# Attention by pairs of heads: two 64-row or two 64-column products at a time, values unsplit float32, scores in float32r from the ninth pair on

## The chip, the cores and the metric

The kernel runs on one core of a Trainium2 chip. The metric is the device time of one execution in microseconds (us), the median of several runs. In the rows below PE is the matrix engine (TensorE), PEld its loads of stationary operands, DVE the vector engine, ACT the scalar engine, POOL the GpSimd engine and SP the engine that issues the DMAs.

## What is computed

Attention over 4 batches of 8 heads, 576 positions of 64 elements, with a mask in blocks of 64, and then two feed-forward layers on the 2304 tokens. The second and third step are not touched by the change.

```python
scores = scale * np.matmul(q, k.transpose(0, 1, 3, 2))
mask = block_i >= block_j                      # blocks of 64 positions
attn = softmax(np.where(mask, scores, -1e9))
x = np.matmul(attn, v)                         # heads side by side: 2304 x 512
x = (silu(x @ w_gate) * (x @ w_val)) @ w_out   # 512 -> 1536 -> 512
out = elu(x @ w_in) @ w_out2                   # 512 -> 2048 -> 512
```

## The kernel before

The tokens are cut into nine chunks of 256. Chunk 0 holds the first 64 positions of each batch; each other chunk holds 256 query positions of one batch (`ORDER`). With g = 0 a chunk's queries see 320 keys, with g = 1 they see 576, so the 32 pairs of heads of chunks 1 to 8 are 16 pairs of the short kind (g = 0) and 16 of the long kind (g = 1), by turns four and four.

PE takes operands in two types here: float32, for which the trace shows two loads and two matmul records for each product, and float32r, for which it shows one. A float32r product keeps fewer bits, so a number is split into a high float32r part and the float32r rest, and the parts are multiplied separately (`mm3` is the three-product form of the feed-forward layers, L183 to L185).

**Attention of one head** (`a_head`) before. Heads 0 to 7 (`fp`) use float32: scores on 64 rows of the array (L476), values on 64 columns (L590, and L614 for the last 64 keys). Heads 8 to 63 use float32r on the whole array: the high part and the rest of the keys are stacked in the 128 rows (`ks`), so that two products, with `qh` and `ql`, make a score block (L478, L479); the high part and the rest of the values stand side by side in the 128 columns (`vs`), so that two products, with the parts `th` and `tl` of the transposed probabilities, make a values step of 128 keys (L592, L593), and one product the last 64 keys (L616). A block of scores is masked, its maximum taken, exponentiated and divided by its sum (DVE, ACT); the probabilities are transposed on PE (L575, L576, L603) and copied out by ACT (L580), split on DVE (L584). `xb`, `xf`, `xh` and `xl` add the two halves of the result and split them for the next layer.

**What runs beside it.** `gv_pair` is the first feed-forward layer of a chunk: 12 slices of 24 products of 256 columns (L183 to L185, written `gv`). Its weights are read as raw words and converted by `conv_unit` on ACT, DVE and POOL. From about 490 us on the other layers follow (`y`, then `h` and `o`).

**What sets the order.** Every step is a task with a guessed duration and a priority; `Plan.order` runs a list schedule over them and emits the instructions of each engine in the order that it finds. Each engine then runs its own list strictly in that order. A task has a `whole` mark: where PE changes between marks, the plan adds `SWITCH` ns to the task and holds the change back by `STAY`. `UNIT0`, `UNIT`, `LEAD1`, `LEAD2` and `LEAD` set when chunks and their heads fall due. `NFILL` zero products (L274) fill PE at the start.

Of the kernel before, what the change touches and what calls it, by code (L numbers as in the profile page):

```python
# [8 lines left out]
F32 = mybir.dt.float32  # L9
# [25 lines left out]
UNIT0, UNIT, LEAD1, LEAD2, LEAD, CLEAD, CSTEP = 3.4, 3.4, 35.0, 10.0, 22.0, 16.0, 1.0  # L35
GF, NACT, NFP, XLP = 4, 48, 8, False
NPOOL = ()
# [4 lines left out]
STAY, SWITCH, HOLD = 30.0, 100.0, 250.0  # L42
# [86 lines left out]
def attention_moe_moe_kernel(ctx: ExitStack, tc: tile.TileContext,  # L129
                             q0, k0, v0, qf, kf, qt, kt, va, vb, wg, wv, wo, w2i, w2o, out):  # L130
# [82 lines left out]
    def sc_lo():  # L213
        return at_ps.tile([128, 512], F32, tag="slo", name="slo")

    def sc_hi():
        return at_ps.tile([128, 2, 512], F32, tag="shi", name="shi")

    cur = {}

    def tr_t():
        cur["tr"] = at_ps.tile([128, 512], F32, tag="tr", name="tr", bufs=2)
        return cur["tr"]

    def pv_t():
        return at_ps.tile([128, 512], F32, tag="pv", name="pv")


    plan = Plan(dict(raw=3, rawb=2, c=4, rk=2, rq=2, rv=2, ks=3, qh=2, ql=2, vs=3, nm=3, sm=3, pl0=2, pl1=2, ph=2, th=3, tl=3,
                     tt=2, xb=2, xf=2, x=3, slo=1, shi=1, tr=2, pv=1, gv=2, th1=2, s2=2, st=2,  # L230
                     ar=5, ah=3, y=6, ys=4, ws=NW, wm=3, gp=NP, et=2, hc=4))
# [3 lines left out]
    pl_t = {g: [attn.tile([128, e], F32, name=f"pl{g}{i}") for i in range(2)] for g, e in ((0, 256), (1, 512))}  # L235
    ph_t = [attn.tile([128, S], F32, name=f"ph{i}") for i in range(2)]
# [32 lines left out]
    def t0_fill():  # L269
        zeros = [nc.const_aps.tensor(0.0, (128, n), F32).bitcast(F32R) for n in (128, 256)]  # L270

        def fill():
            t = cur["tr"] if "tr" in cur else tr_t()
            pe.matmul(t[:, 256:512], zeros[0], zeros[1], start=True, stop=True)  # L274

        add("DVE", 300, lambda: None, PT0 - 1, writes=[("wt", 0, 0)])
        for n in range(NFILL):
            add("PE", 107, lambda n=n: [fill() for _ in range(1 if n else 3)], PFILL, [("wt", 0, 0)])
# [4 lines left out]
    def t0_init():  # L283
# [4 lines left out]
        for i in range(2):  # L288
            add("POOL", 190, lambda i=i: pool.memset(pl_t[0][i][:, 192:256], 0.0), PT0, writes=[("plz", 0, i)])
            add("POOL", 190, lambda i=i: pool.memset(pl_t[1][i][:, 448:512], 0.0), PT0, writes=[("plz", 1, i)])  # L290
# [17 lines left out]
    def t0_attn(s, q):  # L308
        tag = ("slo", "pv", "shi", "shi")[2 * s + q]
        sc_k, tr_k, pv_k = (tag, plan.count["shi"] if s and q else nxt(tag), q), ("tr", nxt("tr"), 0), ("gv", nxt("gv"), 0)  # L310
        st, hs, n = {}, range(4 * q, 4 * q + 4), f"0{s}{q}"

        def qk():
            if s == 0:
                t = (sc_lo, pv_t)[q]()
            else:
                if "t" not in t0_sc:
                    t0_sc["t"] = sc_hi()
                t = t0_sc["t"][:, q]
            st["sc"] = t[:, 0:256].rearrange("p (h k) -> p h k", h=4)  # L320
            for h in hs:
                pe.matmul(st["sc"][:, h % 4], qz[s][:, h], kz[s][:, h], start=True, stop=True)
# [75 lines left out]
    NH = B * 2 * H  # L398
    raws, xfs = {}, {}

    def a_pair(n, prio):
        b, g = ORDER[n // H]
        h, i = n % H, n // 2
        ext, nf = (320, 2) if g == 0 else (576, 4)
        fp = n < NFP

        def lk():
            t = raws.setdefault(i, {})[0] = attn.tile([128, 2, S], F32, tag="rk", name="rk", bufs=2)
            if fp:
                sp.dma_start(out=t[:, 0, 0:ext], in_=kf[h // 2])  # L410
            else:
                sp.dma_start(out=t[:, :, 0:ext], in_=kt[b, :, h:h + 2, 0:ext])

        def lq():
            t = raws.setdefault(i, {})[1] = attn.tile([128, 2, QW], F32, tag="rq", name="rq", bufs=2)
            if fp:
                sp.dma_start(out=t[:, 0], in_=qf[h // 2])
            else:
                sp.dma_start(out=t, in_=qt[g, b, :, h:h + 2])

        def lv():
            rv = raws.setdefault(i, {})[2] = attn.tile([128, 5, 128], F32, tag="rv", name="rv", bufs=2)
            sp.dma_start(out=rv[:, 0:nf + 1], in_=(va, vb)[g][b, h // 2])

        add("SP", 450, lk, prio, [], [("rk", i, 0)], data=500 if fp else 3.0 * ext)
        add("SP", 450, lq, prio, [], [("rq", i, 0)], data=420 if fp else 730)
        add("SP", 450, lv, prio, [], [("rv", i, 0)], data=200 * (nf + 1))

    def a_head(n, prio):
        b, g = ORDER[n // H]  # L430
        h, j, i = n % H, n % 2, n // 2
# [3 lines left out]
        K = {k: (k, n, 0) for k in ("ks", "qh", "ql", "vs", "nm", "sm", "tt", "xb")}  # L435
        K["ksl"], K["vsl"] = ("ks", n, 1), ("vs", n, 1)
        rk, rq, rv = ((k, i, 0) for k in ("rk", "rq", "rv"))

        def new(k, *shape, bufs, dt=F32R):
            st[k] = attn.tile(list(shape), dt, tag=k, name=k, bufs=bufs)  # L440
            return st[k]

        def p_ks():
            act.copy(new("ks", 128, S, bufs=3)[:, 0:ext], raws[i][0][:, j, 0:ext])  # L444

        def p_ksl():
            pool.tensor_tensor(st["ks"][64:128, 0:ext], raws[i][0][64:128, j, 0:ext], st["ks"][64:128, 0:ext].bitcast(F32), ALU.subtract)  # L447

        def p_qh():
            act.copy(new("qh", 128, QW, bufs=2), raws[i][1][:, j])  # L450

        def p_ql():
            pool.tensor_tensor(new("ql", 128, QW, bufs=2), raws[i][1][:, j], st["qh"].bitcast(F32), ALU.subtract)

        def p_vs():
            act.copy(new("vs", 128, 5, 128, bufs=3)[:, 0:nf + 1, 0:64], raws[i][2][:, 0:nf + 1, 64 * j:64 * j + 64])  # L456

        def p_vsl():
            v = st["vs"][:, 0:nf + 1]
            pool.tensor_tensor(v[:, :, 64:128], raws[i][2][:, 0:nf + 1, 64 * j:64 * j + 64], v[:, :, 0:64].bitcast(F32), ALU.subtract)  # L460

        fp, us = n < NFP, slice(64 * j, 64 * j + 64)
        if not fp:
            add("ACT", .833 * ext + 93, p_ks, prio, [rk], [K["ks"]])
            add("POOL", 2.1 * ext + 250, p_ksl, prio, [rk, K["ks"]], [K["ksl"]])
            add("ACT", 307, p_qh, prio, [rq], [K["qh"]])
            add("POOL", 790, p_ql, prio, [rq, K["qh"]], [K["ql"]])
            add("ACT", .833 * 64 * (nf + 1) + 93, p_vs, prio, [rv], [K["vs"]])
            add("POOL", 2.1 * 64 * (nf + 1) + 230, p_vsl, prio, [rv, K["vs"]], [K["vsl"]])
        qk_in = [rk, rq] if fp else [K["ks"], K["ksl"], K["qh"], K["ql"]]  # L470
        v_in = [rv] if fp else [K["vs"], K["vsl"]]

        def qk(v, t, o, w):
            qs = slice(128 * t, 128 * t + 128)
            if fp:
                pe.matmul(v, raws[i][1][us, 0, qs], raws[i][0][us, 0, o:o + w], start=True, stop=True)  # L476
            else:
                pe.matmul(v, st["qh"][:, qs], st["ks"][:, o:o + w], start=True, stop=False)  # L478
                pe.matmul(v, st["ql"][:, qs], st["ks"][:, o:o + w], start=False, stop=True)  # L479

        slo, shi = ("slo", nxt("slo"), 0), ("shi", nxt("shi"), 0)

        def nm_t():
            if "nm" not in st:
                new("nm", 128, 2, bufs=3, dt=F32)
            return st["nm"]

        def sm_t():
            if "sm" not in st:
                new("sm", 128, 2, bufs=3, dt=F32)  # L490
            return st["sm"]

        def qk_lo():
            sc = st["slo"] = sc_lo()[:, 0:e0]
            qk(sc, 0, 0, e0)

        def qk_hi():
            sc = sc_hi()
            if e1 <= 512:
                vw, st["ax"] = [(sc[:, 0, 0:e1], 0)], AXX  # L500
                st["shi"] = sc[:, 0, 0:e1]
            else:
                w = e1 // 2
                vw, st["ax"] = [(sc[:, u, 0:w], w * u) for u in range(2)], AXXY
                st["shi"] = sc[:, :, 0:w]
            st["hi_end"] = vw[-1][0]
            for v, o in vw:
                qk(v, 1, o, v.shape[-1])

        def mask(v):  # L510
            w = v.shape[-1]
            dve.memset(v[0:64, w - 64:w], NEG)

        def mx(u):
            v, ax = (st["slo"], AXX) if u == 0 else (st["shi"], st["ax"])
# [661 lines left out]
```

## Time and profile before

| | |
|---|---|
| median of 3 runs | 1021.86 us (1021.21 to 1023.21) |
| the profiled execution, its own time | 1022.86 us |
| its span, first to last instruction | 1021.1 us |
| PE busy | 1010.5 us (99%), 6542 matmul records |
| DVE busy | 742.6 us (73%) |
| ACT busy | 652.6 us (64%) |
| POOL busy | 285.2 us (28%) |
| granted clock of PE | 1.00 of full speed in the whole span |

A matmul's duration in the profile covers its way through the array: a `gv` product of 256 columns is shown as 0.28 us long, while the next one starts 0.11 to 0.12 us after it. What a product costs PE is therefore read from one start to the next, not from its duration, and a wait shorter than the overlap doesn't show as idle time.

### The profile page before, as it was taken

The page shows a single profiled execution, that of the slowest core. Times are in us where ns is not written, and L with a number is a line of the kernel's source. Part 1 is how long each engine was busy: PE and PEld are TensorE (multiplying, and loading weights), DVE is VectorE, ACT ScalarE, POOL GpSimd, SP SyncE. Part 2 cuts the span into 40 slices and gives each one's busy share as a digit, 9 for nine tenths or more (in the row PEclk, how much of TensorE's full clock was granted, in tenths as well). Part 3 has the DMA queues.
Part 4 walks back from the last instruction along what each step waited for, and adds up shares of the span by engine and source line. Part 5 has one row for each costly group of instructions (what it writes and reads, how often), then busy time and mean ns, then how long its engine had stood idle before and what let it go on. Part 6 is the DMA issues. An engine that isn't in the chain of part 4 may idle for free.

```text
span 1021.1 us, 19137 instructions
## 1 busy us (share of the span) xinstructions
PE 1010.5 (99%) x6542; PEld 930.3 (91%) x6542; DVE 742.6 (73%) x1813; ACT 652.6 (64%) x1645; POOL 285.2 (28%) x291
## 2 busy tenths in 40 slices
PE   9999999999999999999999999999999999999998
PEld 7789999999999999999888889889889989899997
DVE  7899988777777788878766955786986454754554
ACT  6898889888888677653455554655564444654443
POOL 3467535433443344323333322232200000000000
PEclk9999999999999999999999999999999999999999
DMA  6766454323432343015797886887656334353431
GB/s 215 237 209 222 151 180 151 102 84 104 135 115 73 105 125 101 32 64 176 254 340 261 296 323 232 268 264 219 203 155 200 120 114 124 117 176 121 122 105 62
DMA packets 90896, 169.94 MB, mean 166 GB/s; under 512 B 9008, under 2 KB 35120, under 8 KB 90800
## 3 DMA queue, kind: packets, MB, share of 16 engines
q1 hardware_dynamic: 90800, 168.73, 51.5%
q8 instruction: 52, 0.85, 0.4%
q14 instruction: 44, 0.36, 0.1%
HBM read 130.42 MB, written 38.27 MB: 165 GB/s over the span
## 4 chain that ended last, share of the span: by engine, by line
PE 82%; DVE 8%; ACT 4%; DMA 3%; issue 2%; SPq 0%; ACTq 0%; DVEq 0%
PE gv L183 8%; PE gv L184 8%; PE gv L185 7%; PE o L939 6%; PE o L937 6%; PE o L938 6%; PE h L183 5%; PE h L185 5%; PE h L184 5%; PE y L184 5%; PE y L185 5%; PE y L183 5%; PE pv L593 2%; PE pv L592 2%; PE tr L575 2%
## 5 line engine op out<-in xcount | busy, mean ns | idle before, releaser
L183 PE MATMUL gv<-xh,wh 128*128 128x256 f32 x864 | 255.3, 296 | 0.6 <-DVE as L687 0.4
L184 PE MATMUL gv<-xl,wh 128*128 128x256 f32 x864 | 241.3, 279 | 0.0
L185 PE MATMUL gv<-xh,wl 128*128 128x256 f32 x864 | 241.0, 279 | 0.0
L183 PEld LDWEIGHTS gv<-xh,wh 128*128 128x128 f32 x864 | 162.9, 189 | 4.2 <-issue 2.5
L184 PEld LDWEIGHTS gv<-xl,wh 128*128 128x128 f32 x864 | 163.2, 189 | 0.2
L185 PEld LDWEIGHTS gv<-xh,wl 128*128 128x128 f32 x864 | 162.9, 188 | 0.0
L183 PE MATMUL h<-yo,ws 128*128 128x384 f32 x336 | 113.8, 339 | 2.6 <-ACT ys L902 1.2
L185 PE MATMUL h<-yo,ws 128*128 128x384 f32 x336 | 112.8, 336 | 0.0
L184 PE MATMUL h<-yo,ws 128*128 128x384 f32 x336 | 112.7, 335 | 0.0
L898 DVE TENSOR_TENSOR ys<-h,ys 128x384 f32<-128x384 f32 x72 | 40.0, 555 | 68.6 <-ACT ys L902 42.9
L184 PE MATMUL y<-al,woh 128*128 128x512 f32 (+1 forms) x240 | 88.2, 367 | 0.0
L185 PE MATMUL y<-ah,wol 128*128 128x512 f32 (+1 forms) x240 | 88.2, 367 | 0.0
L183 PE MATMUL y<-ah,woh 128*128 128x512 f32 (+1 forms) x240 | 88.2, 367 | 0.0
L848 POOL TENSOR_TENSOR wm<-c,wm 128x256 fp32r<-128x256 f32 x56 | 51.2, 922 | 127.6 <-ACT wm L845 127.5
L891 DVE SCALAR_TENSOR_TENSOR ar<-ar,ar 128x384 f32<-128x384 f32 x96 | 56.5, 589 | 35.3 <-ACT ar L890 34.8
L902 ACT COPY ys<-h 128x384 f32<-128x384 f32 x72 | 34.3, 476 | 74.4 <-PE h L185 73.9
L584 DVE TENSOR_TENSOR tl<-tr,th 128x256 fp32r<-128x256 f32 x176 | 68.9, 415 | 12.0 <-ACT th L580 11.6
L460 POOL TENSOR_TENSOR vs<-rv,vs 128x320 fp32r<-128x320 f32 (+1 forms) x56 | 43.4, 777 | 122.2 <-ACT vs L456 88.6
L889 ACT ACTIVATE ar<-ys 128x384 f32<-128x384 f32 x72 | 37.8, 526 | 59.6 <-DVE ys L898 34.6
L183 PEld LDWEIGHTS h<-yo,ws 128*128 128x128 f32 x336 | 63.1, 188 | 12.1 <-DVE ys L898 3.2
L447 POOL TENSOR_TENSOR ks<-rk,ks 64x576 fp32r<-64x576 f32 (+1 forms) x56 | 68.6, 1226 | 16.4 <-ACT ks L444 7.0
L580 ACT CAST th<-tr 128x256 fp32r<-128x256 f32 x176 | 60.3, 377 | 17.9 <-PE tr L576 16.2
(156 smaller groups left out, 2737.8 us busy)
## 6 DMA issues: line engine op xcount, KB each, us to landing
ws<-w_scr SPq DMA_DIRECT2D x168, 256.0 KB, 2.6
w_scr<-wm SPq DMA_DIRECT2D x56, 256.0 KB, 3.9
a_scr<-as SPq DMA_DIRECT2D x54, 256.0 KB, 2.5
ar<-a_scr SPq DMA_DIRECT2D x48, 256.0 KB, 4.7
rk<-in_kt_dram SPq DMA_DIRECT2D x16, 576.0 KB, 4.1
raw<-in_w2i_dram SPq DMA_DIRECT2D x16, 512.0 KB, 5.3
raw<-in_w2o_dram SPq DMA_DIRECT2D x16, 512.0 KB, 5.1
rq<-in_qt_dram SPq DMA_DIRECT2D x28, 256.0 KB, 3.6
```

The lines of the kernel that those rows point to most:

```text
L183: pe.matmul(dst, wh, xh, start=start, stop=False, skip_group_check=more)
L184: pe.matmul(dst, wh, xl, start=False, stop=False, skip_group_check=more)
L185: pe.matmul(dst, wl, xh, start=False, stop=stop, skip_group_check=more)
L447: pool.tensor_tensor(st["ks"][64:128, 0:ext], raws[i][0][64:128, j, 0:ext], st["ks"][64:128, 0:ext].bitcast(F32), ALU.subtract)
L460: pool.tensor_tensor(v[:, :, 64:128], raws[i][2][:, 0:nf + 1, 64 * j:64 * j + 64], v[:, :, 0:64].bitcast(F32), ALU.subtract)
L580: act.copy(st["th", c], st["tr", c][:, 0:QW])
L584: dve.tensor_tensor(st["tl", c], st["tr", c][:, 0:QW], st["th", c].bitcast(F32), ALU.subtract)
L848: add("POOL", 1000, lambda: pool.tensor_tensor(wm[n][:, 1], part(*x), wm[n][:, 0].bitcast(F32), ALU.subtract), prio, [ck(*x), hk] + whole, ...
L891: add("DVE", 575, lambda: dve.scalar_tensor_tensor(t(), e(), 1.0, t(), ALU.add, ALU.mult), PMP, [tk, ek], [tk])
L937: pe.matmul(d, h, OH[f], start=(p == 0 and u < 2), stop=False)
L938: pe.matmul(d, h, OL[f], start=False, stop=False)
L939: pe.matmul(d, l, OH[f], start=False, stop=(p == HP - 1 and u > 1))
```

## The change

Attention is done by pairs of heads, head 0 of a pair in rows or columns 0 to 63 of the array, head 1 in 64 to 127, their products by turns.

- Keys, queries and values of a pair are loaded once, the two heads over each other (64 rows each) or side by side (64 columns each). The doubled keys and queries in DRAM go.
- **Scores** (`qk` in `a_pair`): for pairs 0 to 7 one float32 product for each block and head; from pair 8 on (`QS`) three float32r products (`qh*kh`, `qh*kl`, `ql*kh`), all on 64 rows. A pair's scores are one task: 4 products (short) or 6 (long) of float32, 12 or 18 of float32r. The blocks of the long kind are 512, 64 and 448 columns wide, of the short kind 320 and 192.
- **Values** (`pv` in `a_pair`): float32 for all pairs, on 64 columns, 6 (short) or 10 (long) products in one task. The last step has 128 columns and covers 128 keys, of which the first 64 meet zeros.
- The splits of the values (`vs`) and of the transposed probabilities (`tl`, `tt`), and `xb` and `xf`, go; keys and queries are split once for a pair. The division by the sum goes from ACT (heads 0 to 47) to DVE. Two steps of transposed probabilities are copied out at once (512 columns).
- Buffers: scores in `sa` and `sb` (1024 columns each), transposes and values share `tp` (two of 512).
- The numbers of the plan: `UNIT` 3.4 to 3.6, the leads, `STAY` 30 to 10. Transposes now come after all the zero products.

```diff
-UNIT0, UNIT, LEAD1, LEAD2, LEAD, CLEAD, CSTEP = 3.4, 3.4, 35.0, 10.0, 22.0, 16.0, 1.0
-GF, NACT, NFP, XLP = 4, 48, 8, False
+UNIT0, UNIT, LEAD1, LEAD2, LEAD, CLEAD, CSTEP = 3.6, 3.6, 25.0, 40.0, 40.0, 20.0, 0.8
+GF, NACT, NTH, QS, NRV = 4, 0, 6, 8, 3
-STAY, SWITCH, HOLD = 30.0, 100.0, 250.0
+STAY, SWITCH, HOLD = 10.0, 100.0, 250.0
...
+        pieces = [(0, 1, 0, 320), (320, 0, 0, 192)] if g == 0 else [(0, 1, 0, 512), (512, 1, 512, 64), (576, 0, 0, 448)]
...
+            for t, (at, q, o, w), j in [(t, p, j) for p in pieces for t in range(len(terms)) for j in range(2)]:
+                us, qs, (x, y) = slice(64 * j, 64 * j + 64), slice(128 * q, 128 * q + 128), terms[t]
+                pe.matmul(sc[j][:, at:at + w], raw[x][us, qs], raw[y][us, o:o + w], start=t == 0, stop=t == len(terms) - 1)
+
+        terms, qk_in = [("rq", "rk")], [rk, rq]
+        if i >= QS:
+            terms, qk_in = [("qh", "kh"), ("qh", "kl"), ("ql", "kh")], [(x + y, i - QS, 0) for x in "qk" for y in "hl"]
...
+        add("PE", (.8334 * len(terms) if i >= QS else 1.667) * (e0 + e1) / (2 if i >= QS else 1) + 45, qk, d0, qk_in, sks, whole="q")
...
+            for c in range(nf + 1):
+                for j, h in enumerate(heads):
+                    x, at, o = (h["th", c // 2], 256 * (c % 2), 0) if c < nf else (st["tt"], 128 * j, 128)
+                    pe.matmul(st["pv"][64 * j:64 * j + 64, o:QW], raw["rv"][:, c, 64 * j:64 * j + 64], x[:, at:at + QW - o], start=c == 0, stop=c == nf)
...
+        add("PE", 427 * nf + 225, pv, d1, [rv, ttk] + [k for h in heads for k in h["thk"]], [pvk], whole="v")
-                pe.matmul(v, st["qh"][:, qs], st["ks"][:, o:o + w], start=True, stop=False)
-                pe.matmul(v, st["ql"][:, qs], st["ks"][:, o:o + w], start=False, stop=True)
...
-                    pe.matmul(st["pv"][:, 0:QW], st["vs"][:, c], st["th", c], start=(c == 0), stop=False)
-                    pe.matmul(st["pv"][:, 0:QW], st["vs"][:, c], st["tl", c], start=False, stop=False)
...
-                        pe.matmul(st["pv"][:, 128:QW], st["vs"][:, nf], st["tt"], start=False, stop=True)
```

On PE, where the attention of the second batch's first heads stands (chunk 3, float32r in both kernels), the list before has the products of single heads (`slo` and `shi` scores, `pv` values) in small groups between `gv` products, all on the whole array:

```order
L592 MATMUL pv<-th,vs 128x256
L593 MATMUL pv<-tl,vs 128x256
L575 MATMUL tr<-ident,pl_125 128x128
L576 MATMUL tr<-ident,ph_127 128x128
L575 MATMUL tr<-ident,pl_125 128x128
L576 MATMUL tr<-ident,ph_127 128x128
L478 MATMUL slo<-ks,qh 128x192
L479 MATMUL slo<-ks,ql 128x192
L183 MATMUL gv<-xh,wh_1_1015 128x256
```

Now, on PE at the same place, a pair's values (L465, two 64-column halves) and the next pair's scores (L429, two 64-row halves) stand as one block between `gv` products:

```order
L184 MATMUL gv<-xh,wl_1_520 128x256
L465 MATMUL tp<-th,rv 64x256 x4
L465 MATMUL tp<-tt,rv 64x128 x2
L429 MATMUL sb<-kh,qh 128x320 x2
L429 MATMUL sb<-kl,qh 128x320 x2
L429 MATMUL sb<-kh,ql 128x320 x2
L429 MATMUL sb<-kh,qh 128x192 x2
L429 MATMUL sb<-kl,qh 128x192 x2
L429 MATMUL sb<-kh,ql 128x192 x2
L182 MATMUL gv<-xh,wh_1_519 128x256
```

The values of a pair became one task that needs the transposed probabilities of both heads, and the array's shape changes three times around the block (whole, 64 columns, 64 rows, whole). In the whole list values and the next scores stand together like this for 22 of the 32 pairs; for the others `gv` products or transposes stand between them.

At the start (chunk 1, float32 in both) PE's list before has a head's values (L590, L614) and another head's scores (L476) in three shapes of the array:

```order
L185 MATMUL gv<-xh,wl_1_92 128x256
L590 MATMUL pv<-th,rv 64x256 x2
L614 MATMUL pv<-tt,rv 64x128
L476 MATMUL slo<-rk,rq 128x192
L476 MATMUL shi<-rk,rq 128x320
L183 MATMUL gv<-xh,wh_0_93 128x256
```

And now at the start on PE a pair's scores and another pair's values:

```order
L429 MATMUL sb<-rk,rq 128x320 x2
L429 MATMUL sb<-rk,rq 128x192 x2
L465 MATMUL tp<-th,rv 64x256 x4
L465 MATMUL tp<-tt,rv 64x128 x2
```

The two heads of the pair stand next to each other in every product, and the last values step has the shape of the others. Counted over the whole list, the array's shape (64 or 128 rows by 64 or 128 columns, transposes taken as whole) changes 45 times before, all among heads 0 to 7, and 105 times now: 32 times to 64 columns, 32 times to 64 rows (22 of these straight from 64 columns) and 41 times back to whole, in all pairs.

## Rows read from the trace of the kernel before

**Rows 1.** Page, busy us, share of the span and records of each engine.
```profile
PE 1010.5 (99%) x6542; PEld 930.3 (91%) x6542; DVE 742.6 (73%) x1813; ACT 652.6 (64%) x1645; POOL 285.2 (28%) x291
```
**Rows 2.** Stages: busy us of each engine, clock, DMA share, GB/s.
```profile
25.00:75.00 50.00, 49.16 (x324) 38.66 (x324) 43.45 (x126) 45.52 (x127) 26.85 (x22) 1.00 0.70 228
185.00:450.00 265.00, 264.80 (x2229) 263.18 (x2228) 204.51 (x684) 202.79 (x592) 96.10 (x108) 1.00 0.31 95
```
**Rows 3.** Waits of PE: who waited for whom, us, times, longest.
```profile
PE h L183 <- ACT ys L902: 1.2, 2, 0.6
...
PE slo L478 <- ACT pl L529: 0.2, 1, 0.2
```
**Rows 4.** PE in order of time (start, length): float32r scores, long kind, one head.
```profile
125.74 0.36 PE L478 MATMUL slo<-ks,qh 128*128 128x448 f32 x1
125.94 0.37 PE L479 MATMUL slo<-ks,ql 128*128 128x448 f32 x1
...
126.68 0.28 PE L183 MATMUL gv<-xh,wh 128*128 128x256 f32 x1
126.80 0.28 PE L184 MATMUL gv<-xl,wh 128*128 128x256 f32 x1
```
**Rows 5.** PE in order of time: float32r scores, short kind, one head.
```profile
235.41 0.25 PE L478 MATMUL slo<-ks,qh 128*128 128x192 f32 x1
...
235.78 0.30 PE L479 MATMUL shi<-ks,ql 128*128 128x320 f32 x1
235.93 0.28 PE L183 MATMUL gv<-xh,wh 128*128 128x256 f32 x1
```
**Rows 6.** PE in order of time: two float32r values steps; then a last step.
```profile
370.13 0.28 PE L592 MATMUL pv<-th,vs 128*128 128x256 f32 x1
...
370.61 0.28 PE L183 MATMUL gv<-xh,wh 128*128 128x256 f32 x1
...
231.38 0.22 PE L616 MATMUL pv<-tt,vs 128*128 128x128 f32 x1
...
231.64 0.31 PE L479 MATMUL shi<-ks,ql 128*128 128x320 f32 x1
```
**Rows 7.** PE in order of time: float32 values of one head, scores of another.
```profile
36.82 0.28 PE L185 MATMUL gv<-xh,wl 128*128 128x256 f32 x1
37.03 0.43 PE L590 MATMUL pv<-th,rv 128*64 128x256 f32 x1
37.30 0.38 PE L590 MATMUL pv<-th,rv 128*64 128x256 f32 x1
...
37.73 0.38 PE L590 MATMUL pv<-th,rv 128*64 128x256 f32 x1
38.04 0.43 PE L614 MATMUL pv<-tt,rv 64*64 64x128 f32 x2
38.40 0.59 PE L476 MATMUL slo<-rk,rq 64*128 64x192 f32 x2
...
39.45 0.39 PE L183 MATMUL gv<-xh,wh 128*128 128x256 f32 x1
39.68 0.28 PE L184 MATMUL gv<-xl,wh 128*128 128x256 f32 x1
```
**Rows 8.** PE in order of time: float32 products of 64 columns, whole array.
```profile
4.65 1.00 PE L322 MATMUL slo<-kz,qz 128*128 128x64 f32 x8
5.49 1.06 PE L322 MATMUL pv<-kz,qz 128*128 128x64 f32 x8
```
**Rows 9.** PE in order of time: transposes between `gv` products.
```profile
41.28 0.27 PE L575 MATMUL tr<-ident,pl 128*128 128x128 f32 x1
41.39 0.27 PE L576 MATMUL tr<-ident,ph 128*128 128x128 f32 x1
```
**Rows 10.** Groups of instructions: shape, count, busy us, mean ns, idle before.
```profile
L176 ACT CAST wh<-c 128x512 fp32r<-128x512 f32 x24 | 15.1, 627 | 1.4 <-DVE c L173 1.4
L584 DVE TENSOR_TENSOR tl<-tr,th 128x256 fp32r<-128x256 f32 x176 | 68.9, 415 | 12.0 <-ACT th L580 11.6
```

## What the change will do to the time

> **What bounds the kernel now.** I read the page's busy times first. PE is busy for 1010.5 of 1021.1 us, the other engines for 28 to 73% [rows 1]. The stages say the same of attention: PE has 264.8 of 265 us between 185 and 450 us and 49.2 of 50 between 25 and 75, at a granted clock of 1.00, the 2.4 GHz level, while ACT and DVE reach some 90% in the early stretch and 77% later [rows 2]. Then the list of PE's waits: eleven rows from 1.2 down to 0.2 us, 6.2 us together, 2.5 of them in the layer `h` that comes after attention [rows 3]. So the matrix engine is the bound from one end to the other, and the time moves by what the change adds to or takes from PE's own list. What happens on ACT, DVE and POOL pays only through the few microseconds of waits.
>
> Because a record's length covers the way through the array, I read each price from one start to the next. A `gv` product costs 0.12 (126.68 to 126.80) [rows 4].
>
> **What goes.** For float32r heads (8 to 63): the scores of a long head are six products, 125.74 to 126.68, 0.94 us [rows 4]; of a short head four, 235.41 to 235.93, 0.52 [rows 5]. Two values steps of 128 keys take 370.13 to 370.61, so 0.24 each; the last step and a score product of 320 columns take 0.26 together, the latter alone 0.15 [rows 5, 6], which leaves 0.11. A short pair costs 2 x (0.52 + 0.48 + 0.11) = 2.22, a long pair 2 x (0.94 + 0.96 + 0.11) = 4.02; 12 short and 16 long pairs make 90.9 us.
>
> For the float32 heads (0 to 7): one head's values and another's scores, with four changes of the array's shape, run from the `gv` product at 36.82 to the second one after them at 39.68, 2.86 us, less 0.24 for two `gv` products, 2.62 [rows 7]. Eight of them are 21.0. PE's list has 45 changes there, not 32, since some scores stand apart; at the price found below the other 13 add 2.6. Together 23.6, and attention's products on PE cost 114.5 us now, transposes aside. These stay the same in number (448), 0.11 each [rows 9].
>
> **Prices for the new form.** A float32 product is two records, and two records of 256 columns take 0.43 (37.30 to 37.73), so 0.215 each [rows 7]; by columns that is 0.11, 0.16, 0.27, 0.38 and 0.43 for 128, 192, 320, 448 and 512. A short product can't go below the load of its 128 stationary columns: eight records of 64 columns take 0.84 (4.65 to 5.49), 0.105 each, where the columns alone would take 0.05 [rows 8]. For float32r 448 columns take 0.20 [rows 4], so I estimate 0.23 for 512 by columns; 320 take 0.15 [rows 5], and 192 and 64 take the load's 0.11.
>
> A change of shape: the last values record starts at 37.73, is through at 37.945, and the next shape's first record starts at 38.04, 0.09 later. Back on the whole array the first product takes 39.45 to 39.68, 0.23 in place of 0.12, since its load was not hidden [rows 7]. So 0.20 for a change to a shape with 128 columns. Into 64 columns: from 36.94, where the `gv` product is through, to 37.08, one record before 37.30, 0.14 [rows 7].
>
> **What comes.** The trace before has no two products on different halves of the array next to each other, so whether they overlap is the open price. Its ends: both halves at once, or one after the other. I take the overlap, but staggered. A float32 product's two records follow each other on one half, and the other head's first record stands behind both in PE's list. If records start in the order of the list, the other half begins one record late, and n pairs of products take 2n + 1 record times, not 2n.
>
> The Trainium skill, page "TensorE: Matmul & The Clock Gate", Part 3, says that products on different parts of the array run at the same time, but that matmuls start and end strictly in program order. No row here shows it; by it the stagger stands, and without the order rule the sum would be 10.9 us less.
>
> - Values, staggered: a short pair 5 x 0.215 + 2 x 0.11 = 1.30, a long pair 9 x 0.215 + 2 x 0.11 = 2.16; 16 of each, 55.4 us.
> - Float32 scores (pairs 0 to 7), staggered: short 3 x 0.27 + 2 x 0.16 = 1.13; long 3 x 0.43 + 0.11 + 3 x 0.38 = 2.54; four of each, 14.7.
> - Float32r scores (pairs 8 to 31), one record each, so both heads side by side: short 3 x (0.15 + 0.11) = 0.78, long 3 x (0.23 + 0.11 + 0.20) = 1.62; twelve of each, 28.8.
> - Changes of shape: 105 in the new list, 32 into 64 columns at 0.14 and 73 at 0.20, 19.1.
>
> The sum is 118.0 against 114.5: **+3.5 us**. The products alone gain: 98.9 us in place of some 106 (114.5 less 45 changes at 0.14 to 0.20). But 60 more changes of shape take some 11 us back.
>
> **Other engines, all beside PE.** The splits that go were up to 68.9 us of DVE (`tl`) [rows 10] and like amounts on ACT and POOL; the division by the sum moves from ACT to DVE. I cost all of it at nothing, since PE covers it [rows 2]. What it can give back is at most PE's waits in attention, 3.7 us (6.2 less 2.5) [rows 3].
>
> A new wait can come: a pair's values are one task that needs the copies of both heads' last transposes by ACT, and behind it in PE's queue stand the next pair's scores and all `gv` products. The copy is 512 columns, 0.63 by the nearest row [rows 10], and the tail's copy not longer, together up to 1.26, and the order puts nine to twelve `gv` products, 1.1 to 1.4 us, between. If ACT, 77% busy [rows 2], is at another piece of 0.63, up to 0.6 us of 32 visits stay uncovered, 19 us. Between 0 and 19 I take 0, as the likewise planned waits before are 0.2 to 1.2 us in all [rows 3]. The fewer and shorter loads (SP's queue) hide behind all this.
>
> The sum stands against the profiled execution, 1022.9 us, which is 1.0 above the median: 1022.9 + 3.5 - 1.0 = **1025.4**.
>
> **The rivals.**
>
> *Loads share one path.* If the stationary operands of the two halves load one after the other, as the 0.105 for each load on the whole array suggests [rows 8], every float32r product costs at least 0.11: short scores 12 x 0.11 = 1.32 in place of 0.78, long ones 3 x (0.23 + 0.22 + 0.22) = 2.01 in place of 1.62. Twelve of each, +11.2: 1036.6. If a load moreover waits until the product ahead of it has started, each handover to the other half shows one load (0.05 for values, 0.11 for scores), about +0.15 and +0.35 for the short and long values, +0.2 and +0.3 for float32 scores: 8.0 + 2.0, 1047. For it: no load here runs beside another.
>
> The Trainium skill, page "TensorEngine Tiling (Array Packing)", Key Properties, says that tiles can do loads and matmuls in parallel. No row shows it; by it this rival falls, and +3.5 stands in place of +14.7.
>
> *The halves don't run at once*, the change doesn't do what it says. Values 2.16 and 3.88 (+0.86, +1.72, sixteen each), float32 scores +0.59 and +1.14 (four each), float32r scores twice 0.78 and 1.62 (twelve each): +77, 1102. Against it I have only the code: in scores the halves share no row of the array, in values no column.
>
> *Faster: no stagger.* If the second head's first record starts beside the first head's first, values cost 0.22 less in every pair (7.0) and float32 scores 0.27 and 0.70 less (3.9): -10.9, **1014.5**. It is on this side once the stagger lost is over a third of its price, 3.5 of 10.9. Against it: on the whole array records start in the order of the list in every row here.
>
> *Cover gone.* Values wait for ACT, 0.3 to 0.6 us a pair: 1035 to 1044. It would show as PE's waits on ACT's copies.
>
> **How the numbers follow.** Forecast 0.45, with a spread of 1020 to 1031 for waits given back (3.7) or added (6); one load path 0.20, with waiting loads 0.10; halves not at once 0.07; no stagger 0.13; cover gone 0.05. The range leaves out the halves not at once, half of the waiting loads and the tail of the fastest case: 1013 to 1046. The likeliest case alone spans 1020 to 1031. Within 0.2% (1019.8 to 1023.9, about what a measurement of this kernel can tell from no change) lies the lower part of the forecast, 0.13; under it no stagger and a little of the forecast, 0.18; above, 0.69.
>
> **What would show it.** In the new trace: the second half's record starting one record behind the first's, 0.2 us in values; 0.22 from pair to pair of 256-column records, not 0.43; float32r score blocks of 0.8 and 1.6 us; 0.09 us gaps and unhidden loads at each of some three changes a pair; `gv` still 0.12 apart; PE's waits still under 7 us. I would be wrong if starts of the halves are a whole product apart, if the loads stand 0.11 apart in the score blocks, or if PE is seen waiting for copies.

## The result, and the profile after

The changed kernel takes 1014.79 us in the median (1014.09 to 1015.74, seven runs) against 1023.08 for the kernel before in the same session (1021.21 the fastest of seven). The ratio is 0.9905, with a 95% interval of 0.9875 to 0.9934: it is faster, by some 8 us, where the forecast was 3.5 us slower. Two of the seven runs of before took 1029.36 and 1030.29 us; without them its median is 1022.87. The profiled execution has a span of 1013.1 us against 1021.1, at a granted clock of 1.00.

First the page's line of busy times, after:

```profile
PE 1000.1 (99%) x6718; PEld 898.0 (89%) x6718; DVE 667.3 (66%) x1489; ACT 532.3 (53%) x1241; POOL 178.2 (18%) x173
```

PE is still the bound, with more records than before (6718 for 6542) in less time; beside [rows 1] DVE has lost 75 us, ACT 120 and POOL 107. Two stages, with the columns of [rows 2] (us, then busy us and records of PE, PEld, DVE, ACT, POOL, then clock, DMA share, GB/s):

```profile
25.00:75.00 50.00, 45.66 (x350) 36.04 (x350) 48.87 (x126) 35.43 (x92) 16.77 (x13) 1.00 0.62 203
185.00:450.00 265.00, 264.72 (x2352) 243.82 (x2352) 149.67 (x451) 134.10 (x353) 41.19 (x41) 1.00 0.25 77
```

From 185 to 450 us PE is full as before, and DVE has fallen from 77% to 56%. Between 25 and 75 us it is the other way round: DVE, now with the divisions by the sum, is busy for 48.87 of 50 us, and PE, which waits for it, has fallen from 49.16 to 45.66. The list of PE's waits says the same (who waited for whom, total us, times, longest):

```profile
PE tp L544 <- DVE ph L520: 4.1, 5, 1.5
PE h L182 <- ACT ys L800: 1.2, 1, 1.2
PE gv L182 <- DVE as L585: 0.9, 3, 0.5
PE tp L269 <- PEq L1059: 0.8, 1, 0.8
PE gv L184 <- POOL wl L179: 0.7, 1, 0.7
```

L520 is the division on DVE, and PE's transposes wait for it; 2.8 of the 4.1 us fall between 25 and 75 us, where all of PE's waits come to 4.2 us, 0.8 before. All waits on this list ahead of the layer `h` come to 7.2 us, 3.7 before; those in `h` to 1.4, 2.5 before [rows 3].

**The two halves.** The float32 scores of a long pair, on PE in order of time (start, length, then line, tiles, shape), and the loads of the first product:

```profile
43.70 0.69 PE L429 MATMUL sa<-rk,rq 64*128 64x512 f32 x1
43.70 0.69 PE L429 MATMUL sb<-rk,rq 64*128 64x512 f32 x1
44.23 0.59 PE L429 MATMUL sa<-rk,rq 64*128 64x512 f32 x1
44.23 0.59 PE L429 MATMUL sb<-rk,rq 64*128 64x512 f32 x1
...
45.73 0.33 PE L543 MATMUL tp<-ident,pl 128*128 128x128 f32 x1
```

```profile
43.69 0.18 PEld L429 LDWEIGHTS sa<-rk,rq 64*128 64x128 f32 x1 [0.17 <-issue]
43.70 0.18 PEld L429 LDWEIGHTS sb<-rk,rq 64*128 64x128 f32 x1
```

Both heads' first records start at 43.70, the second ones together at 44.23; the loads start 0.01 apart. Nothing is staggered, though the first head's two records stand ahead of the second head's in the list. From 43.70 to the first transpose are 2.03 us; the forecast's price with a stagger was 2.54 and a change of shape, 2.74.

At 53.67 the second head's buffer `sb` was late (its load waits for ACT, which still reads the scores of the pair before), and the halves part:

```profile
53.67 1.12 PE L429 MATMUL sa<-rk,rq 64*128 64x512 f32 x2
54.62 0.69 PE L429 MATMUL sb<-rk,rq 64*128 64x512 f32 x1
54.63 0.86 PE L429 MATMUL sa<-rk,rq 64*128 64x64 f32 x3
55.15 0.59 PE L429 MATMUL sb<-rk,rq 64*128 64x512 f32 x1
```

The second head's product starts 0.95 us late, and the first head's next products (54.63) start before the second head's second record (55.15), which stands ahead of them in the list.

Values of a long pair between `gv` products:

```profile
192.53 0.28 PE L184 MATMUL gv<-xh,wl 128*128 128x256 f32 x1
192.74 1.95 PE L465 MATMUL tp<-th,rv 128*64 128x256 f32 x16
194.51 0.39 PE L465 MATMUL tp<-tt,rv 128*64 128x128 f32 x4
194.83 0.39 PE L182 MATMUL gv<-xh,wh 128*128 128x256 f32 x1
195.05 0.28 PE L183 MATMUL gv<-xl,wh 128*128 128x256 f32 x1
```

Sixteen records, eight for each half, take 1.77, which is 8 x 0.215 and 0.05 for the first load. From the end of the `gv` product at 192.53 to that of the one at 194.83 are 2.40 us (192.53 to 195.05, less one `gv` of 0.12): 1.94 for the products, 0.14 and 0.20 for the two changes of shape, and 0.12 for the `gv`.

Float32r scores of a long pair, three products for each block:

```profile
187.59 0.49 PE L429 MATMUL sa<-kh,qh 64*128 64x512 f32 x1
187.59 0.49 PE L429 MATMUL sb<-kh,qh 64*128 64x512 f32 x1
...
188.42 0.27 PE L429 MATMUL sa<-kl,qh 64*128 64x64 f32 x1
...
188.53 0.27 PE L429 MATMUL sa<-kh,ql 64*128 64x64 f32 x1
...
189.41 0.33 PE L543 MATMUL tp<-ident,pl 128*128 128x128 f32 x1
```

187.59 to 189.41 are 1.82 us, 1.62 and a change of 0.20; the products of 64 columns stand 0.11 apart, in each half.

**Where the 8 us lie.** The first `h` product and the last `o` product stand on PE, before, at

```profile
639.28 0.34 PE L183 MATMUL h<-yo,ws 128*128 128x384 f32 x1
...
1016.68 0.39 PE L939 MATMUL o<-oh,al 128*128 128x512 f32 x1
```

and after at

```profile
634.02 0.34 PE L182 MATMUL h<-yo,ws 128*128 128x384 f32 x1
...
1008.73 0.39 PE L837 MATMUL o<-oh,al 128*128 128x512 f32 x1
```

So 5.3 us (639.28 to 634.02) are won up to the layer `h`, and 2.7 us more (377.40 against 374.71) in the layers `h` and `o`, whose code the change doesn't touch. These 2.7 are no chance of one execution: the second trace of before has 377.33 us there, and six of the experiments below have 374.71 again.

### The profile page after: what moved, and what is told of

It is laid out like the page before. It is cut to its first block, busy times and chain, and to the rows that moved or that the text cites. A ratio compares the mean times of both kernels' runs of the same rounds, so it can differ in the third digit from the quotient of the medians.

```text
span 1013.1 us, 18475 instructions
## 1 busy us (share of the span) xinstructions
PE 1000.1 (99%) x6718; PEld 898.0 (89%) x6718; DVE 667.3 (66%) x1489; ACT 532.3 (53%) x1241; POOL 178.2 (18%) x173
## 4 chain that ended last, share of the span: by engine, by line
PE 87%; DVE 10%; issue 1%; ACT 1%; DMA 1%; DVEq 0%; ACTq 0%; SPq 0%
PE gv L182 8%; PE gv L184 8%; PE gv L183 8%; PE o L837 6%; PE o L835 6%; PE o L836 6%; PE h L182 6%; PE h L184 6%; PE h L183 6%; PE y L182 5%; PE y L184 5%; PE y L183 5%; PE tp L465 4%; PE sa L429 3%; PE tp L543 2%; PE tp L544 2%
## 5 line engine op out<-in xcount | busy, mean ns | idle before, releaser
L182 PE MATMUL gv<-xh,wh 128*128 128x256 f32 x864 | 251.7, 291 | 1.1 <-DVE as L585 0.9
L580 DVE SCALAR_TENSOR_TENSOR s<-th,gv 128x256 f32<-128x256 f32 x108 | 44.9, 416 | 84.2 <-ACT th L576 83.8
L746 POOL TENSOR_TENSOR wm<-c,wm 128x256 fp32r<-128x256 f32 x56 | 55.4, 995 | 143.3 <-ACT wm L743 142.9
L576 ACT ACTIVATE th<-gv 128x256 f32<-128x256 f32 x108 | 41.7, 386 | 73.8 <-PE gv L184 73.1
L837 PE MATMUL o<-oh,gl 128*128 128x512 f32 x180 | 70.6, 392 | 0.0
L835 PE MATMUL o<-oh,gh 128*128 128x512 f32 x180 | 70.5, 392 | 0.0
```

Of the source, the lines that this page charges most:

```text
L182: pe.matmul(dst, wh, xh, start=start, stop=False, skip_group_check=more)
L576: act.activation(st["th"], st["t"][:, 0], ACTF.Tanh, scale=0.5)
L580: dve.scalar_tensor_tensor(st["s2"], st["th"], 1.0, st["t"][:, 0], ALU.add, ALU.mult)
L746: add("POOL", 1000, lambda: pool.tensor_tensor(wm[n][:, 1], part(*x), wm[n][:, 0].bitcast(F32), ALU.subtract), prio, [ck(*x), hk] + whole, ...
L835: pe.matmul(d, h, OH[f], start=(p == 0 and u < 2), stop=False)
L837: pe.matmul(d, l, OH[f], start=False, stop=(p == HP - 1 and u > 1))
```

## The experiments

Each is the changed kernel with one edit, unless said otherwise. "Over after" is the difference to 1014.79; the ratios are to the kernel before.

**Both halves, one head after the other in the list.** In scores and in values all products of one head come first, then all of the other:

```diff
-for t, (at, q, o, w), j in [(t, p, j) for p in pieces for t in range(len(terms)) for j in range(2)]:
+for t, (at, q, o, w), j in [(t, p, j) for j in range(2) for p in pieces for t in range(len(terms))]:
...
-for c in range(nf + 1):
-    for j, h in enumerate(heads):
+for j, h in enumerate(heads):
+    for c in range(nf + 1):
```

> Only the order of a pair's products changes, in scores and values: all of head 0's first, then all of head 1's, each on its own half as in the changed kernel; the plan's tasks stay as they are. Theory (each half runs its own products in their order and does not wait for the other half's): the halves still overlap as far as the queue of PE reaches, at best 1014 to 1018 us. Rival (products start side by side only because they are neighbours in the list): the halves run one after the other; with values 2.16 and 3.88 us in place of 1.08 and 1.94, and scores doubled likewise, about 1085 us. A time between says how far the queue reaches.

Measured: 1057.12 us, ratio 1.0334 (1.0293 to 1.0375), 42 us over after, between the two theories. The trace shows why. A long pair's float32r scores, nine products of `sa` and then nine of `sb` in the list:

```profile
217.38 0.50 PE L429 MATMUL sa<-kh,qh 64*128 64x512 f32 x1
...
218.33 0.27 PE L429 MATMUL sa<-kh,ql 64*128 64x64 f32 x1
218.34 0.49 PE L429 MATMUL sb<-kh,qh 64*128 64x512 f32 x1
218.44 0.44 PE L429 MATMUL sa<-kh,qh 64*128 64x448 f32 x1
...
218.92 0.36 PE L429 MATMUL sa<-kh,ql 64*128 64x448 f32 x1
...
219.87 0.36 PE L429 MATMUL sb<-kh,ql 64*128 64x448 f32 x1
```

`sb` starts at 218.34, when the sixth product of `sa` has started and three are still waiting (218.44, 218.72, 218.92). So a product can overtake waiting products of the other half, but only three of them: in the scores of all 16 long pairs of this trace exactly three records of the first head are waiting when the second head's first one starts, of six in float32 and of nine in float32r. A strict list would have started `sb` after the ninth, at 218.92, and free halves at 217.38. In the changed kernel the heads go by turns, and a reach of three would cover all that a stagger would have cost.

**Both heads' values on the same 64 columns.** The same products by the same records, on columns 0 to 63 for both heads, one head after the other (and, since the results then lie in other places, two copies each of half the rows in place of one):

```diff
-pe.matmul(st["pv"][64 * j:64 * j + 64, o:QW], raw["rv"][:, c, 64 * j:64 * j + 64], x[:, at:at + QW - o], start=c == 0, stop=c == nf)
+pe.matmul(st["pv"][0:64, QW * j + o:QW * j + QW], raw["rv"][:, c, 64 * j:64 * j + 64], x[:, at:at + QW - o], start=c == 0, stop=c == nf)
```

> Values of both heads of a pair on the same 64 columns (outputs on the same 64 partitions, next to each other), head 0 first; copying out takes two instructions on ACT and DVE each. Nothing else changes. Theory (the overlap of the two halves is what makes the values cheap): each pair's values cost 2.16 or 3.88 us in place of 1.08 or 1.94, sixteen pairs each, +48 us: about 1062. Rival (the gain came from less work on ACT, DVE and POOL, and PE's list had slack): clearly less, under 1030.

Measured: 1064.90 us, ratio 1.0403 (1.0367 to 1.0439), 50 us over after. A long pair's values, PE in order of time:

```profile
189.14 1.94 PE L465 MATMUL tp<-th,rv 128*64 128x256 f32 x8
190.92 0.38 PE L465 MATMUL tp<-tt,rv 128*64 128x128 f32 x2
191.14 1.89 PE L465 MATMUL tp<-th,rv 128*64 128x256 f32 x8
...
193.17 0.50 PE L429 MATMUL sa<-kh,qh 64*128 64x512 f32 x1
```

Each head takes the 2 us that both take together on two halves. This is the overlap of the values by itself, and it is complete. The rival, slack in PE's list, is ruled out.

**DVE work put back.** From pair 8 on, a subtraction as the one removed, with its result not used, for the 144 transposes of 256 columns:

```diff
+for u in range(2 if i >= QS else 0):
+    dve.tensor_tensor(t, st["tr", c][:, us], out["th", c // 2][:, us], ALU.subtract)
```

> The changed kernel with a dead subtraction on DVE for each 256 columns of transposed probabilities of pairs 8 to 31, of the shape and operands of the one that the change dropped (144 of them, some 60 us of DVE between 90 and 450 us); its result is not used. Theory (the gain is PE's shorter list, DVE is beside it there): 1014 to 1017 us. Rival (the gain came from less work on DVE): most of the 8 us come back, 1019 to 1023.

Measured: 1016.77 us, ratio 0.9934 (0.991 to 0.9958), 2.0 over after. The stage:

```profile
185.00:450.00 265.00, 263.76 (x2343) 242.53 (x2343) 188.50 (x563) 131.62 (x348) 38.61 (x40) 1.00 0.24 73
```

DVE does 188.50 us there in place of 149.67, some 39 of the 55 us that it had lost against the 204.51 of before [rows 2], and the time moves by 2. Most of the gain isn't a lighter DVE; it is PE's own list. What ACT and POOL lost was not put back; before, PE was busy for 264.80 of these 265 us beside them [rows 2].

**Division on ACT for the first eight heads.** `NACT` 0 to 8.

> The division of the probabilities of heads 0 to 7 goes back to ACT, the others stay on DVE. Theory (in 25 to 75 us DVE, busy 48.9 of 50 us, is the bound of the changed kernel and PE waits 4.1 us for the divisions): those waits go, 1010 to 1012 us. Rival (the weights' conversion on DVE is the bound there anyway, the wait only moves): 1013 to 1015.

Measured: 1013.27 us (1012.89 to 1013.72), ratio 0.9903 (0.9876 to 0.993), 1.5 under after. The waits of PE:

```profile
PE gv L182 <- DVE as L585: 2.0, 3, 0.9
...
PE tp L465 <- ACT th L548: 1.1, 1, 1.1
...
PE tp L544 <- DVE ph L520: 0.8, 1, 0.8
```

The wait for the division falls from 4.1 to 0.8, and others come in its place: all waits ahead of `h` come to 6.8 us, 7.2 in after, so most of the wait moved, as the rival had it. It is the lowest median of the study; its ratio can't be told from that of the changed kernel.

**More changes of shape.** `STAY` 10 to 0.

> The changed kernel with the plan's reluctance to change the array's shape taken away (STAY 10 to 0): the same products in another order, 125 changes of shape in place of 105. Theory (a change costs what I priced, 0.14 to 0.20 us, on PE's path): 20 more changes, +2.8 to +4.0 us over the changed kernel, some 1017.6 to 1018.8. Rival (with both halves at work a change is nearly hidden, 0.05 us or less): +0 to +1 us, 1014.8 to 1015.8.

Measured: 1020.43 us, ratio 0.9958 (0.9933 to 0.9982), 5.6 over after: above both theories. Windows of 5 us of its trace, and PE at the end of the first:

```profile
115.00:120.00 5.00, 2.68 (x20) 2.46 (x19) 5.00 (x12) 2.66 (x5) 2.55 (x3) 0.90 0.60 210
120.00:125.00 5.00, 5.00 (x36) 4.37 (x37) 4.97 (x15) 1.75 (x7) 0.00 (x0) 0.76 0.25 82
```

```profile
118.30 0.33 PE L544 MATMUL tp<-ident,ph 128*128 128x128 f32 x1 [2.32 <-DVE ph L520]
...
120.10 0.41 PE L183 MATMUL gv<-xl,wh 128*128 128x256 f32 x1
120.31 0.41 PE L184 MATMUL gv<-xh,wl 128*128 128x256 f32 x1
```

In this order PE waits 2.32 us for the division in a stretch in which it has been busy for only 2.68 of 5 us, with transposes alone in its list from 115.70 to 119.03, and then runs at the lower of its two levels, 1.2 GHz: `gv` products stand 0.21 apart in place of 0.12. By the granted clock 0.10 x 5 and 0.24 x 5, 1.7 us, are given away at most. Whether the time lost them isn't shown: the one of the twelve runs at a granted clock of 0.999 took 1020.29 us, and the nine at 0.997 took 1018.41 to 1020.71. All waits listed ahead of `h` come to 8.7 us, 1.5 more than in after. What is left of 5.6 for the 20 changes, all of them back to the whole array (61 for 41), is 4.1 without the waits and 2.4 without waits and clock, 0.21 or 0.12 each: near the theory, above the rival's 0.05, but the order changes too much with the number for a closer price.

**Scores in one float32 product for all pairs.** `QS` 8 to 32.

> The changed kernel with all pairs' scores as one float32 product (QS 8 to 32), no split of keys and queries. By the starts read in the trace of after, a long pair's scores take 1.84 us in float32 and 1.62 in float32r, a short pair's 0.86 and 0.78, all without the load behind them. Theory (no stagger in either form): 12 x 0.22 + 12 x 0.08 = +3.6 us over the changed kernel, less some 1 us for the splits that go from DVE and ACT: 1017 to 1019. Rival (the stagger of the prediction shows in float32, where a product is two records): 12 x 0.92 + 12 x 0.35 = +15 us, 1030.

Measured: 1016.59 us, ratio 0.9919 (0.9892 to 0.9945), 1.8 over after. The stagger's +15 is ruled out; +3.6 less some 1 was a little too much. PE's wait for L520 is 2.6 us in this order, 1.5 less, and the clock stands at 0.66 between 30 and 35 us, 1.7 us given away at most; these two and the 3.6 don't close on 1.8. In the time, then, the three float32r products are worth at most about 2 us against one float32 product, and by the ratios the two kernels can't be told apart; what the products are worth by themselves isn't shown.

**The due times of before.** In the changed kernel:

```diff
-UNIT0, UNIT, LEAD1, LEAD2, LEAD, CLEAD, CSTEP = 3.6, 3.6, 25.0, 40.0, 40.0, 20.0, 0.8
+UNIT0, UNIT, LEAD1, LEAD2, LEAD, CLEAD, CSTEP = 3.4, 3.4, 35.0, 10.0, 22.0, 16.0, 1.0
```

> The changed kernel with the due times of before (UNIT0 3.4, LEAD1 35, LEAD2 10, LEAD 22, CLEAD 16, CSTEP 1.0), all else as changed. PE's list has the same products and 103 changes of shape in place of 105. Theory (the gain is in PE's products; due times move only waits): the changed kernel's time within 3 us, 1012 to 1018. Rival (a part of the gain, above all the 5 us that waits take or give at the start and some 3 us in the later layers, comes from the new due times): 3 to 8 us slower, 1018 to 1023.

Measured: 1014.63 us, ratio 0.9903 (0.9865 to 0.9942), the same as after. Within it two things cancel:

```profile
631.79 0.34 PE L182 MATMUL h<-yo,ws 128*128 128x384 f32 x1
...
1008.13 0.39 PE L837 MATMUL o<-oh,al 128*128 128x512 f32 x1
```

`h` begins 2.2 us earlier than in after, and from there to the last `o` product are 376.34 us, 1.6 more. So 1.6 of the 2.7 us won in `h` and `o` come from the new due times, which cost 2.2 us up to `h`.

**The kernel before, a second trace.**

> The kernel before once more, for a second trace of it. In the first one the layer h (640 to 760 us) has PE busy 117.4 of 120 us and two kinds of waits for ys, 1.2 and 1.1 us; after has 119.1 and one of 1.2. Theory: these waits belong to the order of the kernel before and are there again (PE 117 to 118 of 120, over 2 us of waits for ys). Rival: they are chance of that one execution, and PE is at 119 or more.

Measured: 1023.01 us; the waits of `h` for `ys` are there again, 1.3 us and 1.3, with PE at 117.21 of 120 us between 640 and 760. They belong to the order of the kernel before and are no chance of one execution.

**A lighter DVE, three forms.** Without the addition of 1e-9 to the sums (the first edit), then with `NACT` 8 too, then with the due times of before as well:

```diff
-add("DVE", 70, lambda: rec(0), prio, [sk2], [sk2], both=True)
-add("DVE", 81, lambda: rec(1), prio, [sk2], [sk2])
+add("DVE", 81, lambda: rec(1), prio, [sk2], [sk2], both=True)
```

> The changed kernel without the addition of 1e-9 to a row's sum of exponentials (L512, 64 of them; the sum is at least 1, so the addition changes nothing in float32). In the trace of after, DVE is busy 48.9 of 50 us between 25 and 75 us, 3.8 of them in ten of these, and PE waits there for DVE. Theory (DVE is the bound of that stretch, and what it gets rid of comes back on PE): 2 to 4 us faster than the changed kernel, 1011 to 1013. Rival (the wait moves to ACT or to transfers, as most of it did with the division on ACT): within 1 us, 1014 to 1015.

> As before this one, and the first eight heads' division on ACT too (NACT 8). Theory (two loads taken from DVE, each pays): 1010.5 to 1012.5. Rival (between 25 and 75 us ACT is then the next to be waited for, so the two don't add): no better than the better of the two alone, 1011 to 1013.3.

> As before this one, and the due times of before. With these due times alone the trace showed PE's starts 2.6 us earlier against its list at the end of attention, and 1.7 us later through the layer h. Theory (these two stay as they were): 0.5 to 1.5 us faster than with the new due times, 1009.5 to 1012. Rival (once DVE is lighter the early gain of the old due times is gone and only the loss in the layer h stays): 1 to 2 us slower, 1012 to 1014.

Measured: 1014.40 us (five runs, 1013.85 to 1015.14), ratio 0.9912 (0.9882 to 0.9942); 1014.60, 0.9915 (0.9886 to 0.9945); 1018.35, 0.9952 (0.9931 to 0.9973). The first follows its rival, the other two lie above both of their theories. In the first, DVE is still busy for 48.47 of 50 us between 25 and 75 us; PE's wait for the division (L520) shrinks from 4.1 to 1.9 us and this one grows in its place (0.9 before the edit):

```profile
PE gv L182 <- DVE as L584: 4.0, 6, 1.6
```

In the second, DVE is down to 44.02 of these 50 us and PE up from 45.66 to 47.46, and the time is that of after all the same. In the last, PE waits 3.9 us for the same `as`, 2.3 for `wl` on POOL and 2.8 for `ys` in `h`. Each edit makes the plan emit another order, and the waits of the first 100 us come out at another place; what DVE has less to do doesn't show in the time. Which order would be rid of these waits stays open.

## Why the prediction was wrong

**The step that failed: "If records start in the order of the list, the other half begins one record late".** They don't so start. The second head's first record starts with the first head's first (43.70 and 43.70, 187.59 and 187.59), and products of one half overtake waiting ones of the other (54.63 before 55.15; 218.34 before 218.44). The term of 10.9 us was not there. How far the reach goes the run with one head after the other shows: three waiting records, where the heads by turns need one (the second head's first goes ahead of the first head's second). With the term away the forecast's own prices give 1014.5, the rival "no stagger", and 1014.79 was measured. The evidence that I set against this rival was that records on the whole array keep the order; there the next record has rows and columns in common with the one before, and such rows can say nothing of products that share no row or no column. I gave 0.13 to a case against which no row of such products spoke, and 0.45 to the stagger. For the same reason the sentence under "What sets the order", that each engine runs its own list strictly in order, is too strong for PE.

The rule behind it was that of the Trainium skill, page "TensorE: Matmul & The Clock Gate", Part 3, that matmuls start and end in program order. The rows named here contradict it for products on different halves. The Trainium skill's page "TensorEngine Tiling (Array Packing)", Key Properties, that tiles load and multiply in parallel, agrees with the loads at 43.69 and 43.70.

**The prices held.** A record of 256 columns 0.215 (1.77 for eight and a first load), the load's floor 0.11 (188.42 to 188.53), float32r scores 1.62 (1.82 with a change of shape), a change 0.14 to 64 columns and 0.20 back (2.40 from `gv` to `gv`), `gv` 0.12. The rivals with one load path (0.11 between the halves' loads; 0.01 in the trace) and with halves that don't run at once (the run on the same 64 columns shows what that costs in the values, +50 us) fall. So does "cover gone": in the list of waits of the changed kernel there is none of a values product (L465); single ones, of some 1 us, come up in the runs with a lighter DVE.

**"I cost all of it at nothing, since PE covers it" was wrong for one stretch.** From 25 to 75 us DVE, with the division, was busy for 48.87 of 50 us, PE's waits in this stretch rose from 0.8 to 4.2 us, and those ahead of `h` from 3.7 to 7.2, where I had waits only given back or, at worst, added by ACT's copies. I had read DVE's 43.45 of 50 there [rows 2], and moved the division onto it without adding the two up. But DVE isn't all of it: with eight heads' division back on ACT only 1.5 us came back, since PE then waited for others. For 185 to 450 us the cover held.

**That 1014.5 comes so near the time is luck: errors cancel.** Without the stagger the list gives -7.4 us (3.5 - 10.9). Up to `h` -5.3 was measured, of which the added waits are +3.5; so PE's products there gained some 1.4 us more than my prices say, and no row of mine tells which. Then come 2.7 us in `h` and `o` that the forecast had at zero: 1.6 are the new due times, shown by the run with the old ones; the other 1.1 is open.

**Chances.** The measured time lies in the range, near its lower end, on the side that had 0.18. What set the sign was one unknown of 10.9 us, three times the forecast's distance from no change. With such an unknown the forecast's sign is the chance given to it, and no more.

## What to carry to other kernels

Two products that share no rows or no columns of the array can be counted at the price of one, first record beside first record, if the program's list puts them by turns; one head wholly after the other loses most of it here (+42 us, where no overlap at all was put at some 70). What it costs is the change of the array's shape, 0.14 to 0.20 us each here, so put products of one shape together. And when splits are taken from a vector engine and something else is given to it, add up the busiest stretch, not the whole: here, in 50 us in which DVE was full, PE's waits rose by 3.4 us, against some 8.8 that its products won up to `h`.

## What the runs showed of the hardware

- Products on the two halves start within 0.01 us of each other, and so do their loads (43.69 and 43.70); each half then goes on by itself (54.63 ahead of 55.15).
- A product overtakes waiting products of the other half, but with three of them waiting at most (one head after the other in the list: `sb` started when three of nine `sa` products were left). In the values of a long pair, by the same run, the second head starts 1.35 us after the first, when three of the first head's ten records are left as well.
- After a wait of 2.32 us in a stretch in which PE had been busy for half the time, with transposes alone, PE's clock was at 1.2 GHz for some 3 us: `gv` products 0.21 apart (the run with `STAY` 0). What such a dip costs in the time isn't shown: with DVE work put back, runs at a granted clock of 0.998 took 1016.25 to 1017.03 us and two at 1.000 took 1016.76 and 1016.90.
